# An attention and Fourier-mixing kernel: the second batch's W2 as seven half-size products, and a new order behind the first pairs

## The chip, the cores and the metric

The kernel runs on one core of one Trainium2 chip. Five engines of that core have instruction lists of their own and meet through semaphores: TensorE (PE, with its weight loads shown as PEld), VectorE (DVE), ScalarE (ACT), GpSimd (POOL) and SyncE (SP, which here only starts DMAs). The metric is the device time of one execution in microseconds. Lower is better.

## The reference, cut to what matters

Inputs are q, k, v of shape (4 batches, 8 heads, 768 positions, 64), W1 (512 x 2048) and W2 (2048 x 512), all float32. The first half is block attention: per query, the three best of twelve blocks of 64 keys by the blocks' mean key, plus the query's own block, with a causal mask. The second half mixes with a Fourier transform and runs a two-layer perceptron:

```python
x = attn_out.transpose(0, 2, 1, 3).reshape(B, S, H * D)      # 4 x 768 x 512
X = np.fft.fft(np.fft.fft(x, axis=1), axis=2)
u = x + np.real(X)
mu, var = mean of u, variance of u                             # over the 512 columns
un = (u - mu) / np.sqrt(var + 1e-06)
out = u + np.maximum(un @ w_ch1, 0.0) @ w_ch2
```

What the change touches is the last line for batch 1 (the second of four): the product of the hidden layer (768 x 2048, after the relu) with W2, and the variance that scales it.

## The kernel before, in words

**Tiling.** The eight heads of a batch are worked off in four pairs, so there are 16 pairs P = 0 to 15 and pair P belongs to batch P // 4. When the four pairs of a batch are done, the batch's Fourier mixing and perceptron follow, beside the next batch's pairs. SBUF tiles have tags, and a new tile under a tag takes the old one's place once the old one's readers are done: `nat0{0,1,2}`, `nat1{0,1,2}`, `nat2{0,1}` take the loaded q, k, v; `hT0` to `hT15` the hidden layer, one tile of 128 hidden columns x 768 rows each; `x_b` (two) the attention output; `zw`, `sd`, `unT`, `ty`, `tr` stages of the transform. PSUM is cut into four places of two banks, `ps0` to `ps3`.

**The order is written out.** Nothing schedules the instructions. The string `ORDER` is a list of tokens `name:arguments@place`; the loop at the end of the kernel walks it and calls a function of the dictionary `WORK` for each token, and every engine executes its instructions in the sequence in which the walk issues them. `@n` chooses the PSUM place or the slot of the tile that the token opens; `~` in front takes the token's other engine (`pick(a, b)`). An engine waits at an instruction until its inputs are there and its output's place is free, and everything behind it on that engine waits too. The tokens that matter here:

| token | function, line | engine and work |
|---|---|---|
| `Lq:P`, `Lk:P`, `Lv:P` | `load` | SP: DMA of q, k, v of pair P into a `nat` tile |
| `kc`, `ks`, `kh`, `kb`, `qc`, `qs`, `g`, `gt`, `gu`, `gx`, `go`, `gl`, `gm`, `K` | several | casts, block sums, block scores and the choice of blocks of pair P (all engines); `qs`, `qc`, `vc` have two possible engines |
| `s:P,i` | `s_mm`, L561 and L566 | PE: score tile i (six per pair) into PSUM |
| `e:P,i` | `s_exp`, L583 | ACT: exponential of a score tile into tile `pt` |
| `d:P,i` | `s_sel`, L589 | POOL: causal cut on the diagonal, in place in `pt` |
| `v:P` | `v_mm`, L601 | PE: 42 products of `pt` tiles with v; needs all `e` and `d` of the pair |
| `x:P` | `v_x`, L267 | DVE: division by the row sum into `x_b` |
| `fs`, `fd`, `f`, `fe` | `fold_s`, `fold_d`, `fg`, `fg_edge`, L267 | DVE: the folds that halve the transform; `fe` on ACT or DVE |
| `y`, `m` | `y_mm` L673 and L679, `m_mm` L706 and L707 | PE: the two transforms |
| `ty`, `tr` | `y_copy`, `y_turn` | ACT or DVE: PSUM to SBUF between them |
| `u:b,kp` | `m_u`, L725 | DVE: u = x + transform for row tiles 2kp and 2kp+1, with the row sum |
| `xu`, `xv`, `un` | `m_x`, `m_centre`, `t_copy` | ACT or DVE: centred rows in f16; SP: their transposes by DMA (batches 1 to 3) |
| `bn:b,kt` | `n_stats`, L789 and L790 | DVE: variance of row tile kt |
| `sq:b,kt`, `mn`, `nv`, `nr` | `n_square` L784, `n_mean`, `n_guess`, `n_newton` | ACT: variance as the sum of a square's row; DVE and POOL: 1/sqrt of it |
| `w:b,it` | `w1_mm`, L842 and L844 | PE: W1 for hidden tile it (of 16) |
| `r:b,it` | `w1_relu`, L852 and L854 | ACT, or DVE with `~`: relu into `hT`it |
| `c:b,st,h` | `w2_mm`, L861 | PE: W2 for row tile st, half h of the 16 hidden tiles: 8 products of 512 columns |
| `o:b,st`, `od` | `w2_o`, L867, `w2_out` | DVE: u += c x 1/sqrt(var) (512 columns); SP: DMA to the output |
| `T:n`, `S:b,i,n`, `p:b,n,st`, `po:b,n,st` | `w2_comb`, `h_comb` (both through `tt`, L267), `w7_mm` L1032, `w7_o` L1039 | the seven-product scheme, below |
| `wa`, `ub`, `k`, `zc`, `zr`, `za`, `zm` | `w6_...`, L957 | batch 3's W1 by a seven-product scheme of its own |

**The seven-product scheme.** Batches 2 and 3 (`W7 = (2, 3)`) do W2 in another way. Hidden layer and W2 are cut into 2 x 2 blocks: rows into an upper and a lower set of three row tiles, the hidden dimension into two halves of 8 tiles, the output columns into two halves of 256. With sums and differences of the blocks, seven block products do in place of eight. `T` (POOL or DVE) forms four differences of W2's blocks once; `S:b,i,n` (DVE, or POOL with `~`) forms sum or difference n of the hidden blocks of tile i (32 per batch, 128 x 384 each); `p:b,n,st` is product n for row-tile pair st (8 products of 256 columns into one of two PSUM banks); `po:b,n,st` (DVE) adds a PSUM bank times 1/sqrt(var) to u (128 x 256) after the products of `W7_OUT`. Batches 0 and 1 do W2 directly, with `c` and `o`: 6 row tiles x 16 products of 512 columns each. Batches 0 and 1 also have their variance from `bn`, batches 2 and 3 from `sq`.

Of the kernel before, what the change touches and what calls it, by code (L numbers as in the profile page):

```python
# [12 lines left out]
F16 = mybir.dt.float16  # L13
# [78 lines left out]
W7 = (2, 3)  # L92
# [40 lines left out]
gm:6@2 ty:0,1 d:5,0 s:6,4@2 x:4 Lc:0 d:5,1 e:6,4@0 W:2 s:6,3@0 u:0,2@0 Lq:8@2 m:0,0@3 d:5,5 e:6,3  # L133
vc:5 m:0,1@2 u:0,0@1 xu:0,2 d:5,4 d:6,3 s:6,1@1 kh:7 s:6,5@0 u:0,1@2 e:6,1 v:5@3 e:6,5 ~xv:0,2
xu:0,1 xt:0,2@1 ~xu:0,0 ~xv:0,1 g:7@2 ~un:0,2 ~xv:0,0 xt:0,1@0 gt:7 xt:0,0@2 ~gu:7 un:0,1 s:6,2@1
un:0,0 s:6,0@0 e:6,2 x:5 w:0,1@2 kc:7 gx:7 w:0,8@1 kb:8 ~go:7 d:6,1 qs:7 w:0,5@3 r:0,8 gl:7 ~r:0,1
kc:8 w:0,6@1 gm:7@3 K:7 r:0,5 w:0,0@2 ~r:0,6 Lk:9@1 bn:0,3 w:0,10@3 r:0,0 ks:8 e:6,0 s:7,5@1
w:0,12@2 bn:0,5 e:7,5@1 Lq:9@0 r:0,10 qc:8@0 s:7,4@0 s:7,3@1 ~r:0,12 qs:8 e:7,4 w:0,13@3 bn:0,0
kh:8 Lv:6@0 kb:9 d:6,2 g:8@2 r:0,13 d:6,0 w:0,2@0 Lv:7@1 d:6,4 gt:8 e:7,3 Li:0 pg:0 ks:9 X:0
Lk:10@0 s:7,2@3 bn:0,4 X:1 w:0,7@2 e:7,2 fs:5,0 d:7,4 qc:9@1 r:0,2 d:6,5 w:0,3@1 d:7,5 kh:9 ~gu:8  # L140
r:0,7 d:7,2 gx:8 s:7,0@3 ~vc:6 go:8 gl:8 w:0,15@0 gm:8@0 e:7,0 fs:4,0 r:0,3 g:9@2 d:7,0 v:6@3 gt:9
K:8 r:0,15 gu:9 bn:0,2 ~qs:9 s:7,1@1 gx:9 w:0,11@2 bn:0,1 e:7,1 ~go:9 gl:9 w:0,4@0 gm:9@1 r:0,11
d:7,1 d:7,3 ~vc:7 K:9 w:0,9@1 ~r:0,4 kc:9 Lk:12@2 x:6 s:8,4@2 v:7@0 e:8,4@0 ~r:0,9 s:8,3@3 x:7
w:0,14@2 e:8,3 s:9,5@1 s:9,4@0 ~r:0,14 e:9,5@1 s:8,0@3 s:9,3@1 fs:6,0 e:8,0 nv:0 c:0,0,0@2 fs:7,1
nr:0 e:9,4 fs:7,0 fs:4,1 fs:5,1 fs:6,1 s:8,2@3 fd:6,1 s:8,1@0 e:8,2 fd:6,0 c:0,0,1 fd:7,1 e:8,1
fd:7,0 f:1,2 Lq:10@1 e:9,3 c:0,1,0 f:1,0 fe:1,0 d:8,1 kb:10 s:8,5@3 s:9,2@0 Lq:11@2 ks:10 c:0,1,1
e:9,2 ~fe:1,2 f:1,1 ~fe:1,1 e:8,5 f:1,3 d:9,2 s:9,0@1 o:0,1 Lk:11@1 y:1,0@0 e:9,0 o:0,0 qc:10@0
fe:1,3 y:1,1@3 ~tr:1,0 od:0,1 c:0,4,0@2 Lq:12@0 kh:10 ~ty:1,0 ty:1,1 qc:11@1 ~tr:1,1 g:10@1 kb:12
c:0,5,0 kc:10 qs:11 Lv:8@0 Lq:13@1 gt:10 kb:11 qs:10 s:9,1@0 gu:10 ks:11 m:1,1@3 e:9,1 gx:10
c:0,2,0@1 d:8,0 kh:11 Lk:15@0 kc:12 d:9,5 u:1,1@3 pg:1 ~go:10 d:8,5 d:9,0 gl:10 g:11@0 ~vc:8 d:8,2  # L150
gm:10@2 c:0,5,1 gt:11 xu:1,1 od:0,0 qc:12@0 ~gu:11 d:9,4 Lv:11@1 d:9,3 ks:12 d:8,3 m:1,0@3 d:9,1
gx:11 K:10 kh:12 kc:11 m:1,2@0 go:11 Lv:9@0 c:0,4,1 u:1,2@4 xv:1,1 un:1,1 d:8,4 gl:11 xu:1,2
u:1,0@1 c:0,3,0 ~qs:12 gm:11@3 bn:1,4 K:11 c:0,3,1 xv:1,2 un:1,2 ~xu:1,0 xv:1,0 kb:15 ~vc:9 g:12@0
v:8@3 gt:12 un:1,0 o:0,3 ~gu:12 s:11,2@0 x:8 c:0,2,1 e:11,2@0 o:0,4 Lk:13@2 o:0,5 s:11,3@3 s:11,4@0
o:0,2 e:11,3 v:9@2 fs:8,0 fs:8,1 e:11,4 gx:12 d:11,3 s:10,4@1 x:9 s:10,0@3 d:11,4 Lv:10@0 e:10,4@1
w:1,15@0 Lk:14@1 qc:13@1 e:10,0 s:11,1@2 go:12 gl:12 ks:15 w:1,10@1 e:11,1 fs:9,0 r:1,15 gm:12@0
od:0,4 s:10,2@3 kb:13 Lq:15@2 w:1,4@2 e:10,2 r:1,10 d:10,2 s:10,1@0 ~r:1,4 d:10,4 w:1,2@3 e:10,1
d:11,2 od:0,5 ks:13 d:11,1 Lq:14@0 s:11,5@1 s:11,0@2 bn:1,0 e:11,5 w:1,5@0 e:11,0 d:11,5 kb:14
d:10,0 K:12 r:1,2 s:10,3@1 ~r:1,5 w:1,9@2 kh:13 e:10,3 bn:1,1 ~vc:11 g:13@3 fs:9,1 d:10,3 bn:1,3
s:10,5@0 w:1,1@1 d:10,1 Lv:15@1 e:10,5 kc:13 d:10,5 gt:13 ks:14 d:11,0 w:1,6@0 ~gu:13 qs:13 qc:15@0  # L160
r:1,9 w:1,13@3 r:1,1 gx:13 vc:10 qc:14@1 v:11@2 ~go:13 Lv:13@0 r:1,13 gl:13 od:0,3 r:1,6 od:0,2
# [1008 lines left out]
```

## Time and profile before

| | |
|---|---|
| median of three timed runs | 277.75 us (276.91 to 277.87) |
| the profiled execution | 276.04 us, its span 274.3 us |
| granted TensorE clock of the profiled execution | 0.998 |
| moved by DMA | 33.47 MB, mean 122 GB/s |
| W1 products `h` (L842 and L844) | 384 |
| direct W2 products `c` (L861), batches 0 and 1 | 192 of 512 columns |
| seven-scheme W2 products `cw` (L1032), batches 2 and 3 | 336 of 256 columns |
| score exponentials `e` (L583) | 96, mean 922 ns, 83.7 us of ACT |

A page of the profile gives each engine's busy time over the span; a view by stretches gives the same for a piece of it; the chain of waits follows the work that ended last back from the end; the timeline lists each engine's instructions by start and duration. In a row, `out<-in` names the tiles, `x` counts the instructions, L is the line of the kernel, and what stands behind `<-` with an engine is what the engine had waited for. A matmul row's duration includes waiting in the array's pipeline, so the spacing of many equal ones, taken from the chain, is the better price.

### The profile page before, as it was taken

The page shows a single profiled execution, that of the slowest core. Times are in us where ns is not written, and L with a number is a line of the kernel's source. Part 1 is how long each engine was busy: PE and PEld are TensorE (multiplying, and loading weights), DVE is VectorE, ACT ScalarE, POOL GpSimd, SP SyncE. Part 2 cuts the span into 40 slices and gives each one's busy share as a digit, 9 for nine tenths or more (in the row PEclk, how much of TensorE's full clock was granted, in tenths as well). Part 3 has the DMA queues.
Part 4 walks back from the last instruction along what each step waited for, and adds up shares of the span by engine and source line. Part 5 has one row for each costly group of instructions (what it writes and reads, how often), then busy time and mean ns, then how long its engine had stood idle before and what let it go on. Part 6 is the DMA issues. An engine that isn't in the chain of part 4 may idle for free.

```text
span 274.3 us, 7099 instructions
## 1 busy us (share of the span) xinstructions
PE 266.9 (97%) x2643; PEld 179.0 (65%) x2643; DVE 232.0 (85%) x688; ACT 195.6 (71%) x302; POOL 125.0 (46%) x328
## 2 busy tenths in 40 slices
PE   7999999999999999999999999999999999999994
PEld 4667777765576565566666666465676888656883
DVE  3889899988878898898898876739999888999972
ACT  2899999977997689779979999830768621589200
POOL 5147836545683449515840978060277030066000
PEclk9999999999999999999999999999999999999999
DMA  7999999999999598679440502044300230500015
GB/s 171 266 216 226 196 254 198 182 181 182 179 209 178 80 191 183 146 134 219 96 135 0 115 2 80 0 96 61 115 2 0 57 61 0 194 2 0 2 76 194
DMA packets 121203, 33.47 MB, mean 122 GB/s; under 512 B 113680, under 2 KB 118224, under 8 KB 121168
## 3 DMA queue, kind: packets, MB, share of 16 engines
q1 hardware_dynamic: 116448, 28.56, 48.4%
q0 software_dynamic: 3664, 4.19, 9.5%
q8 instruction: 21, 0.34, 0.5%
q10 hardware_dynamic: 1056, 0.26, 0.4%
q14 instruction: 14, 0.11, 0.2%
HBM read 28.55 MB, written 6.29 MB: 127 GB/s over the span
## 4 chain that ended last, share of the span: by engine, by line
PE 84%; DVE 10%; ACT 2%; DMA 1%; issue 1%; SPq 0%; DVEq 0%
PE c L861 15%; PE h L842 14%; PE cw L1032 13%; PE sc L566 7%; PE h L844 7%; PE k L957 6%; PE av L601 6%; PE tp L337 3%; PE yp L673 2%; PE sc L561 2%; PE mx L707 1%; PE mx L706 1%; DVE u L725 1%; DMA nat<-in_q_dram 1%; PE warmps L1070 1%; ACT pt L583 1%
## 5 line engine op out<-in xcount | busy, mean ns | idle before, releaser
L583 ACT ACTIVATE pt<-sc 128x1024 f16<-128x1024 f32 (+1 forms) x96 | 83.7, 922 | 14.9 <-PE sc L566 12.0
L842 PE MATMUL h<-unT,w 128*128 128x512 f16 x192 | 64.0, 379 | 0.0
L589 POOL TENSOR_SCALAR_AFFINE_SELECT pt<-pt 128x256 f16<-128x256 f16 x96 | 37.3, 411 | 45.0 <-ACT pt L583 44.2
L844 PE MATMUL h<-unT,w 128*128 128x256 f16 x192 | 52.3, 272 | 0.0
L861 PE MATMUL c<-w_sb,hT 128*128 128x512 f16 x192 | 44.4, 379 | 0.0
L854 ACT ACTIVATE hT<-h 128x768 f16<-128x768 f32 x35 | 27.7, 808 | 17.8 <-PE h L844 17.7
L842 PEld LDWEIGHTS <-w 128*128 128x128 f16 x192 | 18.7, 97 | 21.1 <-DVE rcp L612 0.5
L861 PEld LDWEIGHTS <-hT 128*128 128x128 f16 x192 | 18.2, 98 | 20.2 <-issue 0.5
L566 PE MATMUL sc<-qk 96*128 96x512 f16 (+3 forms) x144 | 26.6, 306 | 0.0
L270 POOL TENSOR_SCALAR_AFFINE_SELECT qk<-mt 32x160 f16<-32x160 f16 x72 | 23.3, 344 | 7.3 <-DVE gt L496 3.2
L601 PEld LDWEIGHTS <-pt 128*128 128x128 f16 x672 | 22.1, 97 | 2.8 <-issue 0.5
L601 PE MATMUL av<-v,pt 128*128 128x65 f16 x672 | 23.2, 193 | 0.2
L844 PEld LDWEIGHTS <-w 128*128 128x128 f16 x192 | 18.8, 98 | 3.0 <-issue 0.2
L1032 PEld LDWEIGHTS <-s 128*128 128x128 f16 x192 | 18.8, 98 | 2.6
L270 POOL TENSOR_SCALAR_AFFINE_SELECT qk<-q 64x768 f16<-64x768 f32 (+1 forms) x15 | 12.5, 832 | 15.6 <-DVE q L444 7.7
L1039 DVE SCALAR_TENSOR_TENSOR u<-cw,rt,u 128x256 f32<-128x256 f32 x35 | 16.5, 480 | 3.3 <-PE cw L1032 3.1
L566 PEld LDWEIGHTS <-qk 96*128 96x128 f16 x144 | 13.0, 97 | 8.9 <-issue 0.5
L256 ACT COPY w<-k 128x384 f32<-128x384 f32 x17 | 8.0, 480 | 12.9 <-PE k L957 12.4
L1032 PE MATMUL cw<-w2t,s 128*128 128x256 f16 x144 | 17.2, 273 | 0.0
L267 DVE TENSOR_TENSOR x<-av,rcp 128x768 f16<-128x768 f32 x16 | 15.3, 958 | 0.6
L852 DVE TENSOR_SCALAR hT<-h 128x768 f16<-128x768 f32 x13 | 12.4, 955 | 4.0 <-PE h L844 3.9
L1032 PEld LDWEIGHTS <-hT 128*128 128x128 f16 x144 | 14.1, 98 | 2.4 <-issue 0.2
(201 smaller groups left out, 557.8 us busy)
## 6 DMA issues: line engine op xcount, KB each, us to landing
nat<-in_v_dram SPq DMA_DIRECT2D x16, 384.0 KB, 4.4
out_dram<-u SPq DMA_DIRECT2D x20, 256.0 KB, 2.4
nat<-in_k_dram SPq DMA_DIRECT2D x36, 96.0 KB, 3.1
nat<-in_q_dram SPq DMA_DIRECT2D x36, 96.0 KB, 3.0
nat<-in_k_dram SPq DMA_DIRECT2D x12, 192.0 KB, 3.6
nat<-in_q_dram SPq DMA_DIRECT2D x12, 192.0 KB, 3.7
w_sb<-in_moe_w_ch_dram POOLq DMA_DIRECT2D x2, 1024.0 KB, 12.0
w<-in_moe_w_ch_dram POOLq DMA_DIRECT2D x2, 768.0 KB, 10.1
```

The lines of the kernel that those rows point to most:

```text
L270: nc.gpsimd.affine_select(out=out, in_=in_, pattern=[[0, i] for i in n], base=0, channel_multiplier=0, compare_op=ALU.is_ge, fill=0.0)
L566: nc.tensor.matmul(ps[:, e, co:co + q1 - q0], qk[0:96, e, 1, 128 * jt:128 * jt + 128], qk[0:96, e, 0, q0:q1], start=True, stop=True)
L583: nc.scalar.activation(out=d["pt"][:, o:o + 2 * n].rearrange("p (e c) -> p e c", e=2), in_=d["sc", i][:, :, 0:n], func=AF.Exp, scale=0.125)
L589: nc.gpsimd.affine_select(out=dg, in_=dg, pattern=[[0, 2], [1, 128]], base=0, channel_multiplier=-1, compare_op=ALU.is_ge, fill=0.0)
L601: nc.tensor.matmul(av[:, e, 66 * st:66 * st + 65], pt[:, co:co + 128], vv[:, e, jt, 0:65], start=(cnt == 0), stop=(cnt == 20))
L842: nc.tensor.matmul(hp[:, 0:512], w1s, unT[:, dt, 0:512], start=(dt == 0), stop=(dt == NDT - 1))
L844: nc.tensor.matmul(hp[:, 512:768], w1s, unT[:, dt, 512:768], start=(dt == 0), stop=(dt == NDT - 1))
L854: nc.scalar.activation(out=hT, in_=hp, func=AF.Relu)
L861: nc.tensor.matmul(c_ps[b, g[0]][:, st - g[0], :], h_t[b, it][:, 128 * st:128 * (st + 1)], w2_sb[:, it, :], start=(it == 0), stop=(it == N ...
L957: nc.tensor.matmul(o, x[:, d, :], y[:, d, :], start=(d == 0 and W7_FIRST[n]), stop=(d == 1), skip_group_check=True)
L1032: nc.tensor.matmul(o, x, y, start=(i == 0 and W7_FIRST[n]), stop=(i == 7), skip_group_check=True)
L1039: nc.vector.scalar_tensor_tensor(out=o, in0=c_ps[b, "w", st][:, W7_BANK[n], 0:256], scalar=rt_t[b][:, kt:kt + 1], in1=o, op0=ALU.mult, op1 ...
```

## The change

Batch 1's W2 is done by the seven-product scheme as well. `W7` becomes `(1, 2, 3)`, and a new `WN = (2, 3)` keeps for batches 2 and 3 alone what `W7` had steered besides: normalising from the guess, and the factor `rt` of `w7_o`.

- **Products.** The 12 tokens `c:1,st,h` and 6 `o:1,st` go; 21 `p:1,n,st`, 32 `S:1,i,n` (two of them on POOL) and 21 `po:1,n,st` come. For batch 1 the two row sets are the even and the odd row tiles (`row_tile`, `h_half`); the sum n = 0 is written in place over one of its inputs in `hT`, for all batches, and the sums 1 to 3 of batch 1 lie in tiles under the tags `zw`, `sd` and `unT`, those of batches 2 and 3 in the `pt` tiles (`h_at`).
- **W2's differences.** They are needed for batch 1 already. `T` has seven steps now; their tiles are under `nat00`, `nat01`, `nat02` and `nat12`, and the difference n = 2 overwrites a block of W2 in place. The q loads of pairs 13, 14 and 15 share slot 2 (`Lq:13@2`, `Lq:14@2`, `Lq:15@2`), where they had slots 1, 0 and 2. A sum of batch 3's W1 (`w6_sum`, n = 3) moves to `nat2`.
- **Variance.** Six ACT squares (`sq:1,kt`, output to a scratch tile `sqj`, row sum kept) take the place of the six `bn:1,kt`.
- **Folds.** `fold_s` and `fold_d` take GpSimd where the token has `~`; nine `fs` and one `fd` have it.
- **Order.** From `gm:6` on the string is written anew. Several relus, `qs`, `vc`, `xu` and `ty` tokens change engine with it.

The functions, cut to their core:

```diff
-W7 = (2, 3)
+W7 = (1, 2, 3)
+WN = (2, 3)
...
     def fold_s(b, hp, j):
         tt(sd[:, j, :, cols], x_b[:, 0:3, cols], x_b[:, 3:6, cols],
-           (ALU.add, ALU.subtract)[j])
+           (ALU.add, ALU.subtract)[j], pick(nc.vector, nc.gpsimd))
...
     def n_square(b, kt):
+        if b not in WN:
+            nc.scalar.activation(out=sqj, in_=u_t[b, kt // 2][:, kt % 2, :], func=AF.Square, scale=0.0625,
+                                 bias=nms[b, kt // 2][:, kt % 2:kt % 2 + 1], accum_out=st_t[b][0][:, kt, 1:2])
+            return
...
+    W2T_STEPS = ((0, 0, 6), (0, 6, 8), (1, 0, 4), (1, 4, 8), (2, 0, 8), (3, 0, 2), (3, 2, 8))
+
+    def w2t_at(n, i0, i1):
+        if n == 2:
+            return w2_sb[:, i0:i1, 256:512]
+        k, o = divmod(W2T[n] + i0, 6)
+        if k not in w2t:
+            w2t[k] = npool.tile([128, 6, 256], F16, tag=f"nat{k // 3}{place[0]}", name=f"wt{'abcd'[k]}_0", bufs=1)
+        return w2t[k][:, o:o + i1 - i0, :]
...
+    def row_tile(b, r, st):
+        return 2 * st + r if b == 1 else st + 3 * half(b, r)
+
+    def h_half(b, it, r):
+        h = h_t[b, it]
+        if b == 1:
+            return h.rearrange("p (s r c) -> p r s c", r=2, c=128)[:, r]
+        return h[:, 384 * half(b, r):384 * half(b, r) + 384].rearrange("p (s c) -> p s c", c=128)
+
+    def h_at(b, i, n):
+        if n == 0:
+            return h_half(b, i, 1)
+        if b > 1:
+            w2t_tiles()
+            t, o = (w2p[n - 1], 384 * i) if n < 3 else (w2p[i // 6], 3072 + 384 * (i % 6))
+            return t[:, o:o + 384].rearrange("p (s c) -> p s c", c=128)
+        if n not in h_s:
+            h_s[n] = bpool.tile([128, 3072], F16, tag=("zw", "sd", "unT")[n - 1], name=f"s{n}_1")
+        return h_s[n][:, 384 * i:384 * i + 384].rearrange("p (s c) -> p s c", c=128)
...
     def h_comb(b, i, n):
-        tt(s[:, n, :], in0, in1, ALU.subtract if n else ALU.add, pick(nc.vector, nc.gpsimd))
+        tt(h_at(b, i, n), in0, in1, ALU.subtract if n else ALU.add, pick(nc.vector, nc.gpsimd))
...
     def w7_o(b, n, st):
-        kt = st + 3 * half(b, r)
+        kt = row_tile(b, r, st)
-                                       scalar=rt_t[b][:, kt:kt + 1], in1=o,
+                                       scalar=(rt_t[b] if b in WN else st_t[b][1])[:, kt:kt + 1], in1=o,
```

The order from `g:15` to the third batch's first W1 token, before (with `...` where a stretch is left out):

```
d:12,4 g:15@0 e:13,0 vc:15 y:2,0@2 gt:15 ~tr:2,1 vc:13 Lv:14@1 w:1,11@0 K:14 ~qs:14 Lv:12@0 ~ty:2,0
bn:1,2 s:12,3@3 c:1,0,0@1 gu:15 ~r:1,11 e:12,3 d:13,3 tr:2,0 d:13,0 kc:14 d:13,4 s:13,2@0 d:12,1
nv:1 d:12,5 m:2,0@3 d:12,3 e:13,2 d:13,5 m:2,2@2 d:12,0 kc:15 d:13,2 s:14,2@0 vc:14 u:2,2@0 c:1,1,0
...
s:15,2@3 e:15,1 c:1,4,1 e:15,2 ~xu:2,1 wa:2,0 un:2,1 xu:2,2 s:15,4@0 o:1,4 s:15,5@3 c:1,3,0 wa:0,0
e:15,5 e:15,4 d:15,5 un:2,2 d:15,0 v:14@3 d:15,2 d:15,4 d:15,3 c:1,3,1 d:15,1 x:14 nr:2 un:2,0
fs:12,0 T:0 v:15@0 o:1,2 c:1,5,0 wa:0,1 od:1,4 o:1,3 x:15 c:1,5,1 T:1 w:2,3@3 fs:14,0 fs:14,1
```

and after:

```
s:12,4@0 tr:2,1 y:2,0@1 e:12,4 T:6@2 ty:2,1 s:13,2@2 S:1,7,2 S:1,0,2 g:15@0 ty:2,0 S:1,6,2 s:12,3@3
gt:15 S:1,6,0 ~tr:2,0 S:1,4,2 m:2,0@0 S:1,5,2 S:1,5,0 S:1,1,2 e:12,3 ~S:1,5,1 p:1,0,0@1 u:2,0@2
e:13,2 d:13,5 m:2,2@3 po:1,0,0 ~qs:14 w:1,11@0 d:13,2 u:2,2@0 ~S:1,1,0 s:12,2@2 ~gu:15 S:1,2,2
r:1,11 S:1,3,2 v:13@3 S:1,0,0 e:12,2 S:1,4,0 S:1,7,0 S:1,1,1 p:1,1,0 S:1,3,0 kc:14 S:1,2,0 S:1,3,1
S:1,0,1 p:1,0,2@0 S:1,2,1 po:1,1,0 s:14,2@2 S:1,4,1 S:1,6,1 S:1,7,1 p:1,2,0 e:14,2@1 mn:2,2
po:1,0,2 po:1,2,0 sq:2,5 s:14,0@2 S:1,6,3 p:1,3,0 S:1,4,3 e:14,0 S:1,1,3 S:1,7,3 mn:2,0 p:1,1,2
...
po:1,4,1 sq:2,2 d:14,4 s:15,1@1 x:12 d:14,0 s:15,2@0 e:15,1@0 d:14,2 p:1,6,1 nv:2,1 un:2,0 e:15,2
s:15,0@3 fs:12,0 s:15,4@1 po:1,6,1 e:15,0 v:14@0 e:15,4 ~xu:2,1 d:15,0 s:15,5@2 d:15,2 s:15,3@3
x:14 un:2,1 d:15,4 d:15,1 e:15,5 wa:0,1 e:15,3 d:15,5 wa:0,0 d:15,3 v:15@1 od:1,3 ~fs:13,1 od:1,5
~wa:1,0 od:1,4 w:2,4@0 x:15 od:1,2 nr:2 fs:14,1 w:2,1@2 fs:12,1 r:2,4 fs:15,0 wa:0,2 w:2,15@3
```

More of the change, by code (lines that the diff above doesn't have):

```diff
@@ L138 @@
[L138 to L149, printed above, removed]
@@ L828, in n_newton @@
             rs = rt_t[b] = rt
-        for _ in range(2 if b in W7 else 3):
+        for _ in range(2 if b in WN else 3):
             tt(t2, vr, rs, ALU.mult, po)
@@ L889, in w6_sum @@
         else:
-            w2t_tiles()
-            t = w2p[i0 // 4][:, 4096:5120]
+            k = i0 // 4
+            if ("n", k) not in w6:
+                w6["n", k] = npool.tile([128, 1536], F16, tag=f"nat2{k}", name=f"w6n{k}_0", bufs=1)
+            t = w6["n", k][:, 0:1024]
         o = 128 * (i0 % 4)
@@ new lines, in w2_comb @@
+    def w2_comb(k):
+        n, i0, i1 = W2T_STEPS[k]
+        lo, hi = slice(0, 256), slice(256, 512)
+        b11, b21, b12, b22 = [w2_sb[:, r + i0:r + i1, c] for c in (lo, hi) for r in (0, 8)]
+        out = w2t_at(n, i0, i1)
+        if n == 0:
+            tt(out, b12, b11, ALU.subtract, pick(nc.vector, nc.gpsimd))
+        elif n == 2:
+            tt(out, b22, b12, ALU.subtract, pick(nc.vector, nc.gpsimd))
+        else:
+            src = (b22, None, b21)[n - 1]
+            i = i0
+            while i < i1:
+                m = W2T[(0, None, 1)[n - 1]] + i
+                j = min(i1, i + 6 - m % 6)
+                tt(w2t_at(n, i, j), src[:, i - i0:j - i0], w2t_at((0, None, 1)[n - 1], i, j), ALU.subtract,
+                   pick(nc.vector, nc.gpsimd))
+                i = j
@@ L1019, in w7_mm @@
         o = c_ps[b, "w", st][:, W7_BANK[n], 0:256]
-        rows, low = [slice(128 * k, 128 * k + 128) for k in (st + 3 * half(b, 0), st + 3 * half(b, 1))]
+        rows, low = [slice(128 * k, 128 * k + 128) for k in (row_tile(b, 0, st), row_tile(b, 1, st))]
         lo, hi = slice(0, 256), slice(256, 512)
```

183 lines of the change are left out of this document (93 added, 90 removed).

## The prediction

> **What bounds the kernel now.** First the engine totals of the page, then busy time by stretch, then the chain that ended last.
>
> ```profile
> span 274.3 us, 7099 instructions
> PE 266.9 (97%) x2643; PEld 179.0 (65%) x2643; DVE 232.0 (85%) x688; ACT 195.6 (71%) x302; POOL 125.0 (46%) x328
> ```
>
> The profiled execution took 276.04 us, 1.74 more than its span; the median of the three timed runs, 277.75, is 1.71 above that execution. Sums below are made on 276.04, and 1.71 is added at the end. A half per cent of the median, 1.39 us, is about what a measurement of this kernel can tell from no change, so the bounds are 276.36 and 279.14.
>
> TensorE at 97% needs a second look, because a busy matmul may be a waiting one. The table by stretch (columns: length, then busy us and instructions of PE, PEld, DVE, ACT, POOL, then the granted clock, DMA share, GB/s) and the chain give it:
>
> ```profile
> 95.00:119.00 24.00, 24.00 (x209) 14.06 (x207) 21.73 (x66) 19.56 (x31) 12.99 (x39) 1.00 0.77 157
> 119.00:141.00 22.00, 22.00 (x221) 13.92 (x218) 19.98 (x71) 18.65 (x28) 11.46 (x33) 1.00 0.81 172
> 161.00:167.70 6.70, 6.70 (x79) 4.14 (x78) 4.13 (x23) 6.27 (x9) 4.52 (x19) 1.00 0.01 2
> 167.70:183.80 16.10, 16.10 (x162) 9.44 (x159) 10.77 (x31) 11.97 (x21) 6.85 (x20) 1.00 0.25 67
> 196.70:214.80 18.10, 18.10 (x136) 12.64 (x135) 17.36 (x44) 14.54 (x25) 12.19 (x13) 1.00 0.00 1
> ```
> ```profile
> 108.82 5.18 PE c L861 x24
> ...
> 175.90 0.87 PE sc L566 x6
> 176.77 1.73 PE c L861 x8
> 178.50 0.55 PE sc L566 x4
> 179.04 1.73 PE c L861 x8
> 180.77 1.28 PE av L601 x42
> 182.06 1.73 PE c L861 x8
> 183.78 1.28 PE av L601 x42
> 185.07 3.47 PE c L861 x16
> 188.54 0.38 PE h L842
> ...
> 254.79 15.73 PE cw L1032 x144
> ```
>
> PE stands at the full length of every stretch, at clock 1.00, and the chain goes from one PE piece straight to the next: 24 products of 512 columns in 5.18 us are 0.216 each, 144 of 256 columns in 15.73 are 0.109 each, which is the column count and nothing on top. So from about 56 us to 270 the path is TensorE's own work. DVE and ACT run beside it at up to 96% (17.36 of 18.10 us) and 94% (6.27 of 6.70) without holding it up. That has two consequences: work taken off PE counts in full, and every hole that the new order leaves in PE's list counts in full too.
>
> **What the change takes off PE.** The second batch's W2 was 96 products of 512 columns (six row tiles of 16), 96 x 0.216 = 20.7 us. It becomes 7 products x 3 tile pairs x 8 steps = 168 of 256 columns, 168 x 0.109 = 18.3. Nothing else changes PE's count. **Gain: 2.4 us**, as long as PE stays full.
>
> **What it gives the other engines.** DVE's and ACT's prices are taken from start to start in the timeline, since neighbours overlap by some 0.08 us:
>
> ```profile
> 160.19 0.69 DVE L725 SCALAR_TENSOR_TENSOR u<-mx,x 128x512 f32<-128x512 f32 x1
> 160.80 0.69 DVE L725 SCALAR_TENSOR_TENSOR u<-mx,x 128x512 f32<-128x512 f32 x1
> 214.52 0.36 DVE L267 TENSOR_TENSOR s<-hT,hT 128x384 f16<-128x384 f16 x1
> 214.79 0.35 DVE L267 TENSOR_TENSOR s<-hT 128x384 f16<-128x384 f16 x1
> 264.22 0.87 DVE L1039 SCALAR_TENSOR_TENSOR u<-cw,rt,u 128x256 f32<-128x256 f32 x2
> L867 DVE SCALAR_TENSOR_TENSOR u<-c,rs,u 128x512 f32<-128x512 f32 x12 | 8.6, 742 | 3.5 <-PE c L861 3.5
> L789 DVE BATCH_NORM_STATS2 bst<-u 128x6 f32<-128x512 f32 x12 | 8.1, 677 | 0.0
> L790 DVE BATCH_NORM_AGGREGATE mv<-bst 128x2 f32<-128x6 f32 x12 | 2.2, 182 | 0.4
> ```
>
> DVE gains 30 sums of hidden activations (`S`) at 0.27 = 8.1 us and 21 evictions (`po`) at 0.39 = 8.2; it loses six 512-wide evictions at 0.66 = 4.0, six variances at 0.60 + 0.18 = 4.7, nine folds (same shape as `S`) to POOL, 2.4, and a few relus and copies to ACT, some 4. Net about +1. ACT gains six squares, 4.2 us, and those copies, so goes to about 205 us. POOL gains some 9. In total all of this has room beside PE; it costs nothing where the order covers it. The working that remains is whether it does, place by place, read from the built program's order of each engine.
>
> **The place that isn't covered: `v:15`.** The last pair's attention product `v:15` needs the exponentials `e:15` (ACT) and the diagonal cuts `d:15` (POOL). Before, its last score tile ends at 179.04 and `v:15` starts at 183.78: two halves of `c:1,3` and `v:14` lie between, 4.74 us of other PE work, and 3.47 of `c:1,5` behind it. Those c pieces were the second batch's W2. In the new order that work is done earlier, and `s:15,3` stands directly ahead of `v:15` with nothing between. ACT's list there, from the end of the score tile `s:14,4`, is `e:14,4`, half of `xu:2,2`, `qs:15`, two squares, four `e:15`, half of `xu:2,1`, `e:15,5`, `e:15,3`.
>
> ```profile
> 118.44 1.94 ACT L583 ACTIVATE pt<-sc 128x1024 f16<-128x1024 f32 x2 [1.14 <-PE sc L566]
> 160.42 1.67 ACT L256 CAST qk<-q 64x768 f16<-64x768 f32 x2
> 168.91 0.72 ACT L784 ACTIVATE x<-u,sm 128x512 f16<-128x512 f32 x1
> 169.61 0.72 ACT L784 ACTIVATE x<-u,sm 128x512 f16<-128x512 f32 x1
> 178.20 1.51 ACT L738 ACTIVATE x<-u,sm,rs 128x512 f16<-128x512 f32 x2
> 179.61 1.29 ACT L583 ACTIVATE pt<-sc 128x256 f16<-128x256 f32 x2
> L589 POOL TENSOR_SCALAR_AFFINE_SELECT pt<-pt 128x256 f16<-128x256 f16 x96 | 37.3, 411 | 45.0 <-ACT pt L583 44.2
> ```
>
> From these, an exponential takes 0.92 start to start, the pair of copies 1.65, a square 0.70, an `xu` half 0.70, the short exponential 0.28, and the last counts whole, 1.02: 0.92 + 0.70 + 1.65 + 1.40 + 3.68 + 0.70 + 0.28 + 1.02 = 10.35 us. With 0.41 for `d:15,3` and 0.15 for two hand-overs (an estimate from the gaps of 0.05 to 0.1 between such pieces) it is 10.9. PE's list over the same span is four W2 products (4 x 0.87), `v:12` and `v:14` (2 x 1.28), the six tiles of `s:15` (0.87 + 0.55 + two of 0.43) and the 15 of 42 steps of `v:15` that need no `e:15,3` (0.46): 3.5 + 2.6 + 2.3 + 0.5 = 8.8. So PE stands for 10.9 - 8.8 = **2.1 us**. Its lower bound is what `e:15,3` alone costs with ACT idle: 1.02 + 0.41 + 0.15 - 0.46 = 1.1. Its upper bound, with the third batch's first layer (`w:2,4`, next on PE, fed by transposes that start after `xu:2,1`) late by a further 0.6, is 2.7.
>
> **The start of the second batch's products.** From `g:15` to `p:1,2,0`, DVE has one transpose (0.3), 19 `S`, two pairs of `u` (4 x 0.61) and two `po`: 0.3 + 5.1 + 2.4 + 0.8 = 8.6 us. PE has `s:12,3`, `m:2,0`, `p:1,0,0`, `m:2,2`, `w:1,11`, `s:12,2`, `v:13`, `p:1,1,0`, `p:1,0,2` and `s:14,2`: 0.43 + 0.87 x 3 + 1.30 + 0.43 + 1.28 + 0.87 x 2 + 0.43 = 8.2. And `s:14,0` takes the PSUM place of `s:14,2` with only one product, 0.87 us, between, where the exponential that frees it takes 1.02. Both lists are at or over PE's: **1.0 us**, between 0.4 (the two excesses alone) and 1.8 (two `S` that POOL computes meanwhile hold DVE for 0.7 each, next part).
>
> **The rest.** Elsewhere behind `gm:6` I compared ACT's and DVE's lists with PE's between the same points. Most differ by less than 0.3 us, as they do before; the tightest is `y:1` to `m:1,1`. The q loads of pairs 13 to 15 now share one buffer, since W2's differences take the others; `Lq:15` waits for `qc:14` and has 5.2 us of PE work until its use, against 8 and more for those pairs before. I put 0.4 us on all this, from 0 to 1.0.
>
> **Sum:** 276.04 - 2.4 + 2.1 + 1.0 + 0.4 = 277.1, and with 1.71 for the median **278.8 us**. I forecast that the saving is given back in holes, most of it at `v:15`.
>
> **Rivals.** *The holes shrink* (faster). If ACT is ahead of its list at `v:15` (PE late for other reasons) only the 1.1 us floor stays, and the rest is covered: 276.04 - 2.4 + 1.1 + 1.71 = 276.4; with no hole at all 275.3. For it: DVE and ACT ran at 94 to 96% beside a full PE. Against: ACT's list at `v:15` is in order and starts with what PE itself releases. Chance 0.2, three quarters of it under 276.36.
>
> *POOL's two-input sums hold DVE* (slower). Up to the third batch's first layer POOL ran hardly any tensor_tensor of size; now there are 14 or so (nine folds, one `fd`, two of W2's differences, two `S`). What one does to DVE can be read where POOL had them before:
>
> ```profile
> 196.22 0.56 DVE L267 TENSOR_TENSOR fg<-zw 128x762 f16<-128x762 f16 x1
> 196.94 1.14 POOL L267 TENSOR_TENSOR s<-hT,hT 128x384 f16<-128x384 f16 x1 [11.61 <-ACT hT L854]
> 197.22 1.27 DVE L267 TENSOR_TENSOR fg<-zw 128x762 f16<-128x762 f16 x1
> ```
>
> The same DVE form takes 0.56 alone and 1.27 beside POOL, and ends only 0.4 after POOL's, at 198.49: 0.71 us lost. Six of the new ones stand between the second batch's transforms and `v:15`. It decides once DVE's list is as long as PE's, which it is at `p:1`: beyond what the term above takes, three that reach PE cost 3 x 0.7 = 2.1, giving 281.0; all six 283. Against: five folds stand early, where DVE has room. Chance 0.3. The Trainium skill's page "SBUF — State Buffer", section "SBUF: two separate sides", calls this an exclusive lock between VectorE and GpSimd that is held for the whole instruction. The rows agree, and by that rule each such sum holds a DVE sum for up to its own length, so it speaks against moving folds to POOL.
>
> *The products save less than said.* 256 columns at 0.109 against 512 at 0.216 leave nothing to doubt; no chance of its own.
>
> **How the numbers follow.** The forecast case, chance 0.5, reaches from 277.5 (lower bounds of the three terms: 276.04 - 2.4 + 1.1 + 0.4 + 0 + 1.71 = 276.9, near the first rival, so I start where it ends) to 280.9 (upper bounds: 2.7 + 1.8 + 1.0); a third of it lies over 279.14. So faster by over 0.5%: 0.15; within: 0.05 + 0.34 = 0.39; slower: 0.16 + 0.30 = 0.46. The range 276.1 to 281.6 leaves out some 0.1 on each side: most of the first rival's lower half and the upper third of the second.
>
> **What would show it.** In the new profile PE should idle some 2 us at a weight load of L608 (the attention product) that waits for POOL's cut, just ahead of the third batch's first layer; less than 1 us in the stretch where L1088's products begin; PE's busy time should fall by 2 to 3 us and DVE's stay near 232. Folds on DVE stretched from 0.3 to about 1 us beside POOL's, with PE waiting on DVE, would show the second rival. The forecast is wrong if PE shows no idle at `v:15`, or if PE stands in many places of some tenths each.

## The result, and the profile after

The changed kernel takes 279.25 us (median of 20 executions, 277.28 to 282.39), the kernel before 277.67 (20 executions, 275.94 to 278.94): ratio 1.0066, 95% interval 1.0045 to 1.0087. The comparisons here leave out executions more than 1.5% above the fastest of their kernel. The forecast was 278.8, in 276.1 to 281.6, with slower by over 0.5% as the largest chance. The profiled execution, the fastest of the 20, took 277.28 us; the sum of the prediction for it was 277.1.

The page of the changed kernel, then its table by stretch (columns as in the prediction):

```profile
span 275.6 us, 7316 instructions
...
PE 265.7 (96%) x2715; PEld 186.0 (67%) x2715; DVE 233.8 (85%) x713; ACT 204.5 (74%) x323; POOL 137.6 (50%) x334
```
```profile
161.00:185.80 24.80, 24.36 (x271) 20.23 (x270) 21.23 (x73) 19.75 (x32) 8.02 (x23) 1.00 0.18 39
185.80:190.20 4.40, 1.92 (x46) 1.58 (x45) 2.71 (x5) 1.91 (x4) 3.67 (x7) 1.00 0.49 107
190.20:215.00 24.80, 24.80 (x176) 16.73 (x177) 20.90 (x57) 13.73 (x21) 11.05 (x22) 1.00 0.11 40
```

ScalarE did gain 9 us and VectorE stayed, as worked out; GpSimd gained 12.6 where some 9 had been put. TensorE's busy time fell by only 1.2 us, not by 2 to 3: a matmul's row includes waiting (0.38 us for products that are spaced by 0.216), so short waits count in it as busy time, and the page alone can't show the saving. In the table TensorE lacks 0.4 us up to 185.8 us and 2.5 us between 185.8 and 190.2. That is `v:15`. In TensorE's timeline (in brackets: idle before it, and what ended it):

```profile
185.33 0.71 PE L573 MATMUL sc<-qk 96*128 96x128 f16 x6
185.88 0.47 PE L608 MATMUL av<-v,pt 128*128 128x65 f16 x10
187.77 1.48 PE L608 MATMUL av<-v,pt 128*128 128x65 f16 x32 [1.42 <-ACT pt L590]
190.16 0.38 PE L859 MATMUL h<-unT,w 128*128 128x512 f16 x1 [0.92 <-DVE rcp L619]
```

and in the chain of waits:

```profile
177.34 1.02 ACT pt L590
...
180.66 1.52 ACT x L797 x4
182.18 2.00 ACT pt L590 x3
184.18 0.62 issue
184.80 1.02 ACT pt L590
185.83 0.70 ACT x L746
186.53 0.28 ACT pt L590
...
187.78 0.42 POOL pt L596
188.24 1.01 PE av L608 x27
```

The chain leaves TensorE at 177.34 for ScalarE's list (`e:14,4`, then two squares, the exponentials of pair 15, half of `xu:2,1`), ends in GpSimd's last cut, and comes back at 188.24 with 27 of the 42 steps. From 185.88 to 188.24 TensorE had 15 steps of 0.0305 us to do, 0.46: **1.9 us idle**. The 27 steps end at 189.06, and the third batch's first layer `w:2,4` starts at 190.16: **1.1 us more**. The row names VectorE's `rcp` there, but that had ended at 189.5; what came last was a transpose. SyncE's timeline, and the view of the transposed tile:

```profile
180.29 8.57 SPq L784 DMA_TRANSPOSE unT<-x  x6
```
```profile
L784 SPq DMA_TRANSPOSE unT<-x x6: 1198/1215/2077, 180.3 to 187.7; - x6
DMA to landing us min/median/max: 2.4/2.5/3.9
```

The sixth is issued at 187.7 and lands 2.4 us later, at 190.1. The first could not be issued before 180.3, since batch 1's sums n = 3 lie under the tag `unT` until `p:1,4,1` has read them (it ends at 180.06).

### The profile page after: what moved, and what is told of

Read it like the earlier page. It is cut to its first block, busy times and chain, and to the rows that moved or that the text cites. A ratio compares the mean times of both kernels' runs of the same rounds, so it can differ in the third digit from the quotient of the medians.

```text
span 275.6 us, 7316 instructions
## 1 busy us (share of the span) xinstructions
PE 265.7 (96%) x2715; PEld 186.0 (67%) x2715; DVE 233.8 (85%) x713; ACT 204.5 (74%) x323; POOL 137.6 (50%) x334
## 4 chain that ended last, share of the span: by engine, by line
PE 71%; DVE 16%; ACT 5%; DMA 3%; issue 2%; SPq 1%; POOL 1%; DVEq 0%; POOLq 0%; ACTq 0%
PE cw L1088 17%; PE h L859 14%; PE h L861 7%; PE k L976 7%; PE sc L573 5%; PE av L608 4%; PE c L878 3%; ACT pt L590 3%; PE tp L344 3%; DVE u L733 3%; PE yp L681 2%; PE sc L568 2%; DMA nat<-in_k_dram 1%; DVE x L273 1%; DVE kr L431 1%
## 5 line engine op out<-in xcount | busy, mean ns | idle before, releaser
L871 ACT ACTIVATE hT<-h 128x768 f16<-128x768 f32 x37 | 29.2, 805 | 12.9 <-PE h L861 12.8
L276 POOL TENSOR_SCALAR_AFFINE_SELECT qk<-mt 32x160 f16<-32x160 f16 x72 | 24.1, 356 | 14.8 <-DVE mt L545 5.7
L1088 PEld LDWEIGHTS <-hT 128*128 128x128 f16 x288 | 28.0, 98 | 4.7 <-issue 0.2
L273 POOL TENSOR_TENSOR w2t<-hT 128x384 f16<-128x384 f16 x13 | 12.0, 931 | 27.1 <-PE k L976 17.2
L878 PE MATMUL c<-w_sb,hT 128*128 128x512 f16 x96 | 22.0, 379 | 0.0
L1088 PE MATMUL cw<-w_sb,hT 128*128 128x256 f16 x144 | 17.5, 273 | 0.1
L276 POOL TENSOR_SCALAR_AFFINE_SELECT qk<-q 64x768 f16<-64x768 f32 (+1 forms) x13 | 10.7, 822 | 13.1 <-ACT q L262 7.6
L878 PEld LDWEIGHTS <-hT 128*128 128x128 f16 x96 | 9.0, 97 | 10.3 <-issue 0.5
L568 PE MATMUL sc<-qk 64*128 64x512 f16 (+3 forms) x112 | 14.9, 306 | 0.6 <-ACT pt L590 0.2
```

What stands on the lines that cost most here:

```text
L273: (eng or nc.vector).tensor_tensor(out=out, in0=in0, in1=in1, op=op)
L276: nc.gpsimd.affine_select(out=out, in_=in_, pattern=[[0, i] for i in n], base=0, channel_multiplier=0, compare_op=ALU.is_ge, fill=0.0)
L568: nc.tensor.matmul(ps[:, e, co:co + q1 - q0], qk[hs[e], 1, XW(P), 128 * jt:128 * jt + 128], qk[hs[e], 0, XW(P), q0:q1], start=(co == 0), s ...
L871: nc.scalar.activation(out=hT, in_=hp, func=AF.Relu)
L878: nc.tensor.matmul(c_ps[b, g[0]][:, st - g[0], :], h_t[b, it][:, 128 * st:128 * (st + 1)], w2_sb[:, it, :], start=(it == 0), stop=(it == N ...
L1088: nc.tensor.matmul(o, x, y, start=(i == 0 and W7_FIRST[n]), stop=(i == 7), skip_group_check=True)
```

## The experiments

**The theory**: TensorE's saving is given back in holes that the order leaves, most of it at `v:15`, in two waits, ScalarE's list and then the transposes. There are three rivals: it is ScalarE's list alone; GpSimd's sums hold VectorE; the seven-product scheme itself costs it, not the order. A fourth came up on the way, the clock.

All rows below are of one profiled execution each. Two things vary between executions of one program and have to be kept apart. The start: all kernels with the new order but `folds_dve` are alike up to `v:7`, yet `v:7` began at 82.9 us in the changed kernel and at 86.6 in `direct_w2`. So stretches are measured from `v:7` on. And the granted clock, which comes up below. In the experiments' kernels the line numbers are off by a few: L607 is the attention product, L1087 the seven-scheme product, L858 the first layer.

**Are there two stacked waits?** Three kernels bring ScalarE's list forward, free the transposes' tile sooner, or both.

```diff
 act_ahead
-po:1,6,0 ... p:1,1,1 e:14,3 ... x:13 ... s:14,4@3 ... e:14,4 ... wa:2,0 ... u:2,1@4 ~qs:15 ... v:12@3 ... sq:2,3 sq:2,2 ... s:15,1@1
+po:1,6,0 x:13 ... p:1,1,1 s:14,4@3 e:14,3 e:14,4 ... u:2,1@4 mn:2,1 wa:2,0 ... ~qs:15 sq:2,3 sq:2,2 ... s:15,1@1 ... v:12@3
 turn_early
-p:1,5,1 ... p:1,6,2 ... p:1,4,1 ... e:15,0 v:14@0 e:15,4 ~xu:2,1
+p:1,4,1 p:1,5,1 ... p:1,6,2 ... ~xu:2,1 e:15,0 v:14@0 e:15,4
```

> Changed kernel with ScalarE's list brought forward ahead of the last pair: x:13 earlier on VectorE, so that s:14,4 and its exponential run three tiles sooner; u:2,1 and the two squares behind it earlier; s:15,1 ahead of v:12. The transposes of the third batch are left as they are. Theory of two stacked waits: the hole inside v:15 shrinks from 2.1 us to about 0.5, but w:2,4 behind it still waits for the DMA transposes that land near 190.1 us, which begin only when p:1,4,1 has read the sums under the tag unT; so the idle time moves from v:15 to w:2,4 and the time stays at 1.006 of before (-0.2 us at most). Theory of ScalarE alone: the hole goes and w:2,4 follows, -1.6 to -2.1 us, 0.999 to 1.001 of before.

> Changed kernel with p:1,4,1 ahead of p:1,5,1 and p:1,6,2, so that the tag unT comes free 1.75 us sooner, and the last xu:2,1 half ahead of e:15,0 on ScalarE. Theory of two stacked waits: the hole inside v:15 stays at 2.1 us (the list of ScalarE is as long as it was), the 0.95 us in front of w:2,4 goes, -0.9 us, 1.003 of before. Theory of ScalarE alone: the wait in front of w:2,4 has another cause (x:14 or x:15 on VectorE, as the profile's row names), and nothing changes, 1.006.

> Both edits of the two kernels beside it. Theory of two stacked waits: more than the sum of the two, since each hides the other: of 3.0 us some 0.5 stay, -2.5 us, 0.997 of before, faster than before. Theory of ScalarE alone: the same as the first of the two alone, 0.999 to 1.001.

Measured: 1.0114 (1.0071 to 1.0156), 1.0052 (1.0029 to 1.0076) and 1.0078 (1.0053 to 1.0104). The first and the third came slower than either theory has it; the interval of the second holds both forecasts. In the first, TensorE waits three times for an eviction by VectorE, once behind the earlier `x:13`, once where `s:14,4` no longer lies between two products, and once behind the earlier `u:2,1`, while `v:15` still waits (TensorE's timeline):

```profile
173.64 1.03 PE L1087 MATMUL cw<-w_sb,s 128*128 128x256 f16 x8 [0.79 <-DVE u L1094]
...
180.05 1.03 PE L1087 MATMUL cw<-w_sb,s 128*128 128x256 f16 x8 [0.58 <-DVE u L1094]
...
182.83 1.03 PE L1087 MATMUL cw<-w_sb,s 128*128 128x256 f16 x8 [0.87 <-DVE u L1094]
...
191.43 0.33 PE L607 MATMUL av<-v,pt 128*128 128x65 f16 x5 [1.35 <-ACT pt L589]
```

So my picture of one list was too simple: to run ScalarE ahead, VectorE, the PSUM places and a tile (below) have to be ahead too. The second, 1.0052 against 1.0066, can't be told from the changed kernel. In its profile the first layer does follow `v:15` without a wait, as it does in the third's, so the second wait hung on the start of the transposes (the edit moves both what frees the tag `unT` and `xu:2,1`). But it starts no sooner (107.5 us behind `v:7`, against 107.3): ScalarE's squares now wait 0.85 us for VectorE's mean, and `v:14` and `v:15` wait 0.3 to 0.7 us in four places.

But the table by stretch of the first shows something that no theory had. The third number from the right is the granted clock:

```profile
190.00:192.00 2.00, 0.50 (x11) 0.30 (x9) 1.36 (x3) 1.37 (x3) 1.44 (x4) 1.00 0.50 102
192.00:194.00 2.00, 1.30 (x29) 0.93 (x29) 1.02 (x2) 0.00 (x0) 2.00 (x3) 0.89 0.60 169
194.00:196.00 2.00, 2.00 (x8) 0.96 (x7) 1.88 (x6) 0.00 (x0) 1.54 (x5) 0.50 1.01 382
196.00:198.00 2.00, 2.00 (x11) 1.08 (x10) 0.00 (x0) 0.81 (x1) 1.64 (x6) 0.76 0.14 47
```

Behind the idle stretch the clock is halved for over 3 us: at 194 to 196 TensorE is busy all the time and does 8 products where 14 are usual. From the start of the third batch's first layer to the end of the span it takes 85.4 us in the changed kernel's profile and 86.8 to 87.0 in these three: 1.4 to 1.6 us lost. All three profiles have it; the changed kernel's doesn't, but 12 of its 20 executions were granted 0.987 to 0.994 on average (median 280.25 us) and 8 had 1.000 (median 277.76).

**Do GpSimd's sums hold VectorE (second rival)?** The ten folds go back; the four other large sums of GpSimd stay.

```diff
-~fs:4,1 ~fs:5,1 ~fs:4,0 ~fs:6,0 ~fd:6,1 ~fs:7,0 ~fs:8,1 ~fs:9,0 ~fs:13,1 ~fs:13,0
+fs:4,1 fs:5,1 fs:4,0 fs:6,0 fd:6,1 fs:7,0 fs:8,1 fs:9,0 fs:13,1 fs:13,0
```

> Changed kernel with the nine fs and one fd that it put on GpSimd back on VectorE. Theory of the order: VectorE has room where they stand, no change (1.005 to 1.008 of before). Rival, two-input sums on GpSimd hold VectorE and that reaches TensorE: -0.7 us or more for each hold that reaches it, 1.004 or less.

Measured 1.0112 (1.0083 to 1.0142): not faster, so the rival falls as the main cause. The hold itself is real. In the changed kernel's timelines of GpSimd and of VectorE:

```profile
121.72 1.89 POOL L273 TENSOR_TENSOR sd<-x 128x384 f16<-128x384 f16 x1
```
```profile
122.76 1.06 DVE L273 TENSOR_TENSOR sd<-x 128x384 f16<-128x384 f16 x1
...
124.01 0.31 DVE L273 TENSOR_TENSOR sd<-x 128x384 f16<-128x384 f16 x1
```

VectorE's fold takes 1.06 us beside GpSimd's and 0.31 alone, and ends 0.2 behind it. It is the one place of that kind that I found to reach TensorE, with some 0.28 us ahead of 126.1, where a product waits for the relu behind that fold; in the profile with the folds back that wait is gone. Why the kernel with the folds back is slower was not separated. In its profile the sixth transpose is issued at 188.9 and lands 2.9 us later, and the clock is halved for longer; its TensorE timeline and its table by stretch:

```profile
191.84 0.58 PE L858 MATMUL h<-unT,w 128*128 128x512 f16 x1 [1.75 <-DMA unT<-x]
```
```profile
192.00:194.00 2.00, 2.00 (x7) 0.88 (x6) 1.10 (x3) 0.00 (x0) 1.14 (x5) 0.50 1.00 378
194.00:196.00 2.00, 2.00 (x7) 0.88 (x6) 0.00 (x0) 0.81 (x1) 0.00 (x0) 0.50 0.05 17
```

**Does the idle time lower the clock?** TensorE is given matmuls of zeros to do while it waits, and nothing else moves.

```diff
     def v_mm(P, e):
+        if P == 15:
+            for _ in range(38 if e == 0 else 0):
+                nc.tensor.matmul(av[:, 0, 400:512], wsrc, wsrc[:, 0:112], start=True, stop=True, ...)
```

> Changed kernel with 38 matmuls of zeros (112 columns, some 1.9 us) ahead of v:15, into unused columns of its PSUM tile; nothing else moves. They fill TensorE's idle time and do none of the kernel's work. Theory of the clock: the idle time at v:15 is what lets TensorE's granted clock drop to 0.50 just behind it; filled, the clock stays at 1.000 in nearly all executions, the median falls by 1 to 1.5 us to 277.8 to 278.3 (1.001 to 1.004 of before) and the slowest execution stays below 280, though TensorE still waits as long for the last pair's exponentials. Rival, the clock drops and the scatter have another cause (the loads at the start, chance): more than half of the executions stay at 0.987 to 0.994 and the median at 279 or above.

> Changed kernel with 38 matmuls of zeros ahead of v:15 and 18 more behind it, so that both idle stretches are filled; nothing of the kernel's own work moves. Theory of the clock: at 0.996 or more in 11 of 12 executions (with the first stretch alone filled it was 10 of 12, without filling 8 of 20), median 277.8 to 278.4. Rival, the clock falls by chance: as many low clocks as with the first stretch alone or more, median 278.7 or above.

TensorE's timeline with the first stretch filled:

```profile
186.45 2.03 PE L605 MATMUL av<-zeros 128*128 128x112 f16 x38
188.32 1.50 PE L611 MATMUL av<-v,pt 128*128 128x65 f16 x42
190.32 0.38 PE L862 MATMUL h<-unT,w 128*128 128x512 f16 x1 [0.50 <-DVE rcp L622]
```

Counted from `v:7`, `v:15` ends where it ended and the first layer starts 0.4 us sooner, and the clock is at 0.997 or more in 10 of 12 executions; with both stretches filled it is so in 6 of 7. Together 3 of 19 are low, against 12 of 20 unfilled: the idle time does lower the clock. On the time the forecast was too good: 278.71 us, 1.0061 (1.0027 to 1.0094), no gain over the changed kernel that can be told, and 280.0, 1.0093 (1.0058 to 1.0128). In the second, the first layer starts only at 192.82, with 2.0 us of idle time left behind the second filling; the sixth transpose was issued at 188.5, and landings there took up to 4.2 us. What delayed it was not isolated.

**The scheme or the order?** Batch 1's W2 direct in the new order, and the kernel before with the cover of `v:15` taken away.

```diff
 direct_w2
-p:1,0,0@1 S:1,... po:1,0,0 p:1,1,0 p:1,2,0 ...      (21 p, 21 po, 32 S)
+c:1,0,0@1 ... c:1,0,1 ... o:1,0 ...                 (12 c, 6 o)
 before_tight
-s:15,5@3 c:1,3,0 ... v:14@3 ... c:1,3,1 ... v:15@0
+s:15,5@3 ... v:15@0 c:1,3,0 v:14@3 c:1,3,1
```

> Changed kernel, its order kept, with batch 1's W2 done directly again: c and o at the places of the seven-scheme products and evictions, its S left out, and the in-place step of T for batch 2 moved behind the last c. Variance, folds and order stay. Theory of the order: TensorE has 2.4 us more, the hole at v:15 stays, the first sums' hole (0.8) and the tag unT's delay (0.5) go: 0.8 to 1.7 us over the changed kernel, 1.009 to 1.013 of before. Rival, it is the scheme (its sums and evictions) that gives the saving back and not the order: at or below before, 1.000 or less.

> Kernel before, with one thing moved: v:15 directly behind s:15,5, ahead of c:1,3,0, v:14 and c:1,3,1, so that its cover of 4.7 us is gone. The same work, no seven-scheme for batch 1. Theory of the cover: v:15 waits for the exponential that frees its PSUM place (ends at 180.9) and for the last diagonal cut (182.25), from 178.9 on; TensorE stands for 2.3 us, 1.008 of before, and by the theory of the clock up to 1.015, with granted clocks of 0.987 to 0.994 in a good part of the executions where before has 0.997 to 1.000. Rival: TensorE makes the time up later (the third batch's transposes were late anyway), 1.002 or less, clocks unchanged.

Measured 1.0117 (1.0078 to 1.0155) and 1.0077 (1.005 to 1.0105), both as expected, but low clocks came in only 2 of 8 executions of `before_tight`. The seven products do save TensorE's time: without them the same order takes 1.4 us more from `v:7` to the first layer (108.7 against 107.3), which is 2.4 more of products less 1.0 of waits that go, all waits taken together. And the kernel before loses as much without the change when `v:15` loses its cover (TensorE's timeline of `before_tight`):

```profile
178.91 0.71 PE L565 MATMUL sc<-qk 96*128 96x512 f16 x4
181.53 2.28 PE L600 MATMUL av<-v,pt 128*128 128x65 f16 x42 [1.91 <-ACT pt L582]
```

**Can the order be mended?** The first two kernels rewrite the tokens from `p:1,3,1` to `w:2,12`, the second from the trace of the first. The third also mends two places ahead of them, and the fourth is the second with one of these, `fs:8,1` on VectorE.

```diff
 retune4, from p:1,3,1 on (cuts d, output DMAs od, fs:12,0 and batch 3's sums wa left out)
+qs:15 gm:15@2 xu:2,0 K:15 s:14,4@3 po:1,3,1 e:14,4 p:1,4,1 u:2,1@4 mn:2,1 un:2,0 p:1,6,2 po:1,4,1 xu:2,2 un:2,2 po:1,6,2
+sq:2,3 sq:2,2 v:12@3 nv:2,1 s:15,1@1 e:15,1@0 x:12 s:15,2@0 e:15,2 ~xu:2,1 un:2,1 p:1,5,1 po:1,5,1 s:15,4@1 e:15,4
+s:15,0@3 p:1,6,1 e:15,0 po:1,6,1 s:15,3@0 s:15,5@2 e:15,3 v:14@1 e:15,5 x:14 v:15@3 w:2,4@0
```

> Changed kernel with the order from p:1,3,1 to w:2,12 written anew: u:2,1 right behind po:1,3,1 so that the squares run early, qs:15 on GpSimd, p:1,4,1 directly behind s:14,4 so that the tag unT is free for the transposes, s:15,1 and s:15,2 ahead of v:12, s:15,3 in the PSUM place of s:15,2, v:14 between the last score tile and v:15, e:15,5 as the last exponential. The work is the same. Theory of two stacked waits: the third batch's first layer starts 1.7 to 2.5 us sooner than in the changed kernel, the clock stays at 1.000: 276.4 to 277.2, 0.995 to 0.998 of before. Theory that the saving can't be had behind ScalarE's list at all: 1.004 or above.

> The re-tuned order, mended where its trace showed TensorE waiting: v:12 ahead of s:15,1, because the exponentials of pair 15 write the tile that v:12 reads and so can't begin before v:12 has ended (1.3 us), po:1,4,1 and po:1,6,2 issued ahead of p:1,5,1 (0.7 us), and xu:2,1 two exponentials sooner, so that the last transposes land near 188 us (0.8 us); PSUM places 1 and 3 change names from there on. The work is that of the changed kernel. Theory that the chain squares, v:12, e:15, d:15 and the transposes are what holds: 2.0 to 2.8 us under the re-tuned order, clocks at 0.998 or more, 275.3 to 276.3, 0.992 to 0.996 of before. Rival, the six transposes on the one DMA queue are the next wait and land no sooner: 0 to 0.5 us gained, 1.000 to 1.003.

> As the one beside it, and two more places mended: s:14,0 and s:14,5 one product later, so that the exponential that frees their PSUM place is covered (0.45 us where the sums' products begin), and fs:8,1 back on VectorE (0.28 us that TensorE waited for a relu held behind a fold, itself held by GpSimd's). Theory of the order: a further 0.5 to 0.7 us, 0.990 to 0.995 of before. Rival, the shift only moves the waits: as the kernel beside it.

> The second re-tuned order, with one token changed: fs:8,1 on VectorE instead of GpSimd. A second measurement of that order beside the kernel before. Theory that two sums on GpSimd hold one on VectorE and so the relu behind it: the 0.27 us that TensorE stands at 125.9 us go, the rest stays; 0.994 to 0.997 of before. Rival, the first measurement of that order was lucky in its starts: 0.999 or above.

The first missed its forecast: 1.0026 (1.0001 to 1.0051), 278.06 us. In its profile it saves nothing from `v:7` to the first layer (107.25 us against 107.27), but the idle time lies in several places and the clock stayed at 0.998 or more in all 12 executions; what it gains seems to come from the clock. Its ScalarE timeline shows what the prediction had missed:

```profile
183.57 1.94 ACT L589 ACTIVATE pt<-sc 128x1024 f16<-128x1024 f32 x2 [2.69 <-PE av L607]
```

An exponential waits for an attention product: pair 15's exponentials write the tile `pt` that `v:12` reads. With `v:12` ahead, `v:14` and `v:15` run with 0.24 us of gaps (84 steps of 0.0305 are 2.56 us, and the first layer follows 2.80 after their start), here in TensorE's timeline of the last kernel:

```profile
185.70 2.96 PE L607 MATMUL av<-v,pt 128*128 128x65 f16 x84
188.50 0.39 PE L858 MATMUL h<-unT,w 128*128 128x512 f16 x1
```

The second came as expected, 276.52 us, 0.9958 (0.9933 to 0.9984). The third, 276.60 and 0.9987 (0.9959 to 1.0015), exchanged one wait for another at 162 us; it missed its forecast and can't be told from the second. The last, with `fs:8,1` back on VectorE, took **276.27 us, 0.9961 (0.993 to 0.9993)**, as expected: two measurements of that order, which differ in one token, lie under the kernel before, and its profile lacks the stop ahead of 126.1. From `v:7` to the first layer it takes 105.0 us, against 107.3 in the changed kernel: the same work with the holes at `v:15` closed. It has the lowest median here, though it can't be told from the second.

## Why the prediction was right, point by point

- **What bounds it** (TensorE's own work, every hole in full): right. From `v:7` to `v:15`, all pieces of TensorE's timeline less their own spacing leave some 1.9 us idle in the changed kernel and 0.4 in the kernel before, and the sums fit the span.
- **Gain 2.4**: right; `direct_w2` bears it out, 1.4 us longer with 1.0 us less of waits.
- **Hole at `v:15`, 2.1 (1.1 to 2.7)**: 1.9 inside it and 1.1 behind, together 3.0, just over the upper bound. The larger part came as worked out: ScalarE's list with the last cut takes 10.9 us (177.34 to 188.20), as summed, and TensorE's 9.0, with a wait of 0.3 that the 8.8 did not have. The smaller I had bounded by 0.6 and put down to `xu:2,1`; it was the tag `unT`, held by the sums until 180.06, and six transposes one after another on one queue. And ScalarE's list had a second guard that I hadn't seen, `v:12`, which is one reason why `act_ahead` failed: its exponentials of pair 15 waited 2.05 us for that product.
- **Start of the products, 1.0, and the rest, 0.4**: together 1.4, and 0.9 behind `v:13` and 0.5 more than before ahead of it came. The split was not right: at the start itself one wait stands out, `s:14,0` for its PSUM place as foreseen, 0.46 us from the spacing (TensorE's timeline, below); the excess of VectorE's list shows with 0.2 at most, ahead of `m:2,0`. The rest was larger instead.

```profile
163.06 0.59 PE L573 MATMUL sc<-qk 96*128 96x512 f16 x2 [0.29 <-ACT pt L590]
```

- **Sum for the profiled execution**: 277.1 against 277.28. That they agree so closely is partly luck. The errors cancel: the hole was 0.9 larger, but the stretch behind the first layer was 0.4 us shorter (85.4 against 85.8), and `v:7`, at 82.9 us against 81.8 with three more score tiles (1.3 us) ahead of it, came 0.2 sooner than they account for.
- **The step to the median** was too small: I added 1.71, the distance of before. For the changed kernel it is 1.97, and its median holds executions with a lowered clock, a price that the sum didn't have; the forecast "just within 0.5%" became 0.66%. How much of the 1.6 us between the medians the clock makes stays open. The 8 executions with the clock at 1.000 have a median of 277.76, hardly above the kernel before, which would make it nearly all; but `fill`, with the clock up in 10 of 12, still took 278.71.
- **Rivals**: the holes did not shrink; GpSimd's sums held VectorE for 0.75 us, as priced with 0.71 (1.06 against 0.31), but only one such hold was found to reach TensorE, with 0.28.

## What to carry to other kernels

Where one engine is full, a saving on it is worth only what the holes of the new order leave of it: read what stands between the last producer and its consumer on the full engine, and give every consumer as much other work as its producers' list is long. Before moving a step to fill a hole, list all that its start needs (the tile it writes and who still reads it, the PSUM place, the queue of its DMA), since behind the wait that the trace names stand others that end just ahead of it. When a median moves more than the profile, look at the granted clock of every execution before looking for another wait.

## What the runs showed of the hardware that was not expected

- **The clock falls behind short idle times.** In `act_ahead` no single wait in that stretch was longer than 1.35 us, and 2.7 us of idle time in the 4.0 from `v:15` to the first layer were enough for 0.50 (its rows above). The Trainium skill, "TensorE: Matmul & The Clock Gate", section "Why this matters for your kernels", warns of idle gaps over about 3 us. The rows differ: waits that add up, with thin products between, do it too. Low clocks (0.994 or less) came in 12 of 20 executions of the changed kernel, 3 of 6, 6 of 12 and 7 of 12 of the first three kernels above, 5 of 6 of `folds_dve` (idle 3.8 us), 2 of 8 of `before_tight`, 0 of 6 of `direct_w2` (idle 1.8), 2 of 36 of the last three re-tuned kernels and 1 of 89 of the kernel before: more often, on the whole, with more idle time.
- **The clock changes in steps of 3.41 us.** Three of the four profiles with a halving have it for 3.41 us, and `folds_dve` for twice that, 191.01 to 197.83. In all four it begins a whole number of such steps behind the start of the trace's clock record (in `act_ahead` at 193.55, 55 steps behind 5.82). Cut into these steps, the table of `act_ahead` and then that of the changed kernel:

```profile
190.14:193.55 3.41, 1.33 (x32) 1.09 (x32) 1.79 (x5) 1.23 (x3) 2.85 (x5) 1.00 0.47 101
193.55:196.96 3.41, 3.35 (x11) 1.61 (x12) 2.33 (x6) 0.60 (x1) 2.67 (x11) 0.50 0.78 296
196.96:200.37 3.41, 3.41 (x23) 1.99 (x21) 2.33 (x5) 0.21 (x1) 1.19 (x3) 1.00 0.02 5
```
```profile
184.46:187.87 3.41, 1.99 (x53) 1.74 (x50) 2.17 (x5) 3.25 (x5) 2.10 (x6) 1.00 0.48 96
187.87:191.28 3.41, 2.34 (x39) 1.69 (x39) 1.96 (x5) 0.00 (x0) 3.08 (x8) 1.00 0.68 203
```

  In `act_ahead` the waits fall into one step, which leaves TensorE 2.1 us idle, and the next step is halved; in the changed kernel's profile they are split, 1.4 and 1.1 us, and none is. That may be one reason why the same program is halved in some executions only, but the rule is not settled: counted in the same way, `turn_early` was halved behind a step with 1.5 us idle, and `before_tight` kept its clock behind one with 1.9.
- **Transposes by DMA** take 1.2 us each on SyncE's queue, but single ones took 1.7 to 2.4, and their landing took 2.4 to 4.5 us. What lengthens them stays open.
